# The last copy and the output's DMA move to ScalarE

## The chip, the core and the metric

The kernel runs on one core of one Trainium2 chip. The core has five engines with programs of their own: TensorE (PE in the profile), VectorE (DVE), ScalarE (ACT), GpSimd (POOL) and SyncE (SP). SP computes nothing; here it issues DMAs. Engines wait for each other through semaphores. The metric is the device time of one execution in microseconds (us); lower is better.

## What is computed

Two inputs of 640 values each pass one step of attention with a cached history (32 heads, 4096 positions, 128 values per head) and one feed-forward block, and a gate mixes the two:

```python
g = _sigmoid((x * gate_w).sum(-1, keepdims=True))
q = (x @ wq)                                   # 2 x 32 heads x 128
scores = einsum("bhqd,bhkd->bhqk", q, k_cache) * Dh ** -0.5
a = einsum("bhqk,bhkd->bhqd", softmax(scores), v_cache) @ wo
b = einsum("bsf,fd->bsd", silu(einsum("bsd,df->bsf", x, w1)), w2)
return g * a + (1 - g) * b                     # (2, 1, 640)
```

All is float32. The caches are 2 x 128 MiB; with the weights some 298 MB are read once, and 5 KB are written.

## The kernel before

The work on the caches is cut into 16 items: 8 groups of 4 heads for each of 2 inputs. An item has a K part and a V part of 8 MiB each. On-chip memory holds three such slabs, `a` and `b` for K and `v` for V, and SP issues the loads into them as they come free. For an item, POOL and DVE multiply K by the query, DVE reduces the products to scores and finds their maximum, ACT makes the exponentials, PE multiplies them with V, and DVE and PE bring the sums into the layout that the output projection needs (tile `oP`). After the last V part SP has also issued the loads of `wo` in six pieces (`load_wo`).

The end of the program is short. `in_halves` multiplies the first three quarters of `wo` into one PSUM bank; `merge` copies that bank to on-chip memory on ACT (L568) and adds it into a second bank, `acc`; `in_quarters` (L586) multiplies the last quarter of `wo`, whose pieces land last, into `acc`. Then DVE copies `acc` (160 values on each of 128 partitions) to the tile `ot` (L891), SP issues the DMA of `ot` to the output, and SP waits for its landing (L897). POOL waits until SP says that the DMA is sent and clears the kernel's semaphores (L904, L905).

Every instruction is recorded with what it reads and writes in a small class, `Flow`. `plan` finds for every operation which others it must wait for, and leaves out what its engine knows already through earlier waits. `run` then emits each engine's program in order, so all DMAs have the line of one helper, L69. `repeat` emits some PE work as a loop. `once` wraps a stretch of an engine's operations in a loop that runs one time, with a branch hint at its head; `spans` says which operations of ACT, DVE and PE are wrapped.

Near the start the program writes the output once with zeros: a DMA of 5 KB from the still zeroed tile `oP`, on SP's queue, behind the loads of `w1`, `x`, the gate, `w2` and `wq`. The tile `xz_col`, which the change uses in its place, is zeroed by POOL at L323; DVE later copies the turned input into it (L424).

The program is stored in order for each engine and loaded by DMA in pieces, here called code pages. The trace shows such loads as DMA packets of the kind "instruction".

Of the kernel before, what the change touches and what calls it, by code (L numbers as in the profile page):

```python
# [158 lines left out]
def gated_decode(nc, x, kc, vc, wq, wo, w1, w2, gate, out):  # L159
    P = 128  # L160
# [15 lines left out]
    HB = 16  # L176
    CV = 68
    G = 4
    W = D // G
    W2 = D // 2  # L180
    NP = HQ // 2
    PR = 2 * Q
# [7 lines left out]
    s_out, s_sent = nc.alloc_semaphore("output"), nc.alloc_semaphore("sent")  # L190
    f = Flow(nc)
    V, S_, T_, G_ = nc.vector, nc.scalar, nc.tensor, nc.gpsimd

    def sb(name, shape, align=32):
        return nc.alloc_sbuf_tensor(name, shape, F32, align_bytes=align)[tuple([slice(None)] * len(shape))]

    def bank(name):
        return nc.alloc_psum_tensor(name, [P, 512], F32)[:, :]
# [6 lines left out]
    def part(n, *ks):  # L205
        return [f"{n}.{k}" for k in (ks or range(8))]
# [10 lines left out]
    xz_col = sb("xz_col", [P, J * 32 + 48])  # L217
    xz, col = xz_col[:, : J * 32].rearrange("p (j z) -> p j z", z=32), xz_col[:, J * 32 :]
# [21 lines left out]
    oP, xs = oP_xs[:, : -D // Q], oP_xs[:, -D // Q :]  # L240
# [4 lines left out]
    ps_q, ps_o, ps_v, ps_acc, ps_t, ps_m, ps_0, ps_1 = (bank(f"ps{i}") for i in range(8))  # L245
    oT = ps_m[:64, 256:512].rearrange("p (n r) -> p n r", r=32)
    early, acc = ps_acc[:, :W2], ps_0[:, :W]
# [11 lines left out]
    ot = slab["v"][:, (NP - 1) * PD + W2 :][:, :W]  # L259
# [24 lines left out]
    def load_wo(g):  # L284
# [12 lines left out]
        for k, (c0, c1) in enumerate(zip(cuts, cuts[1:])):  # L297
# [12 lines left out]
        writes=part("v", 0),  # L310
# [7 lines left out]
            out=ident, in_=ident, compare_op=ALU.not_equal, fill=1.0, base=0, pattern=[[-1, P]], channel_multiplier=1  # L318
        ),
        reads=["ident"],  # L320
        writes=["ident"],
# [3 lines left out]
    f.op("POOL", lambda: G_.memset(seq, 0.0), writes=["seq"])  # L325

    out_rows = out.rearrange("b s (n d) -> (s n) b d", n=G)
    f.dma("SP", out_rows, oP[0:P:HB, :W], reads=["oP"], writes=["out"])

    f.op("DVE", lambda: V.memset(ones, 1.0), writes=["ones"])  # L330
    f.op(
# [2 lines left out]
        reads=["ident"],  # L334
        writes=["block"],
# [6 lines left out]
        reads=["block"],  # L342
        writes=["fold"],
# [4 lines left out]
        reads=["ident"],  # L348
        writes=["sel"],
# [4 lines left out]
        reads=["ident"],  # L354
        writes=["half"],
# [9 lines left out]
        reads=["sel"],  # L365
        writes=["pick"],
# [4 lines left out]
        reads=["sel"],  # L371
        writes=["own"],
# [4 lines left out]
        reads=["ident"],  # L377
        writes=["side"],
# [6 lines left out]
        reads=["block"],  # L385
        writes=["spread"],
# [4 lines left out]
        reads=["ident"],  # L391
        writes=["mask"],
    )
    f.op("DVE", lambda: V.memset(join, 0.0), writes=["join"])
    for e in range(2):
# [6 lines left out]
            reads=["ident", "join"],  # L402
            writes=["join"],
        )
        for t in (at, at + 32):
# [3 lines left out]
                reads=["ident", "join"],  # L409
                writes=["join"],  # L410
# [10 lines left out]
        reads=["xs0", "xs1"],  # L421
        writes=["xt"],
# [5 lines left out]
        reads=["xt"],  # L428
        writes=["gx"],
# [7 lines left out]
    for b in range(B):  # L437
        for j in range(J):
# [12 lines left out]
                reads=part("a") + ["xt"],  # L451
                writes=[f"hsum{b}"],
            )

    def mm_hr():
# [18 lines left out]
        reads=["ones", "gp"],  # L474
        writes=["ps_o"],
# [7 lines left out]
        reads=["g"],  # L483
        writes=["gc"],
# [7 lines left out]
    for e in range(2):  # L492
# [3 lines left out]
            reads=["ps_v"],  # L496
            writes=[f"spaced{e}"],
# [8 lines left out]
        reads=["he", "gc"],  # L506
        writes=["he"],
    )
    for e in range(2):
# [5 lines left out]
            reads=["he", "turned", "half", "seq"],  # L515
            writes=[f"seq{e}"],
# [63 lines left out]
    def in_quarters(g):  # L580
        for k in range(PR):
            at = LEAD + 32 * (g * PR + k)

            def fn(k=k, at=at):
                for n in range(G):
                    last = T_.matmul(  # L586
                        acc[32 * n : 32 * n + HB + 1, :],
                        oP[:, at : at + HB + 1],
                        slab["b"][:, k * D + n * W : k * D + (n + 1) * W],
                        start=False,  # L590
                        stop=(k == PR - 1),
                    )
                return last

            f.op("PE", fn, reads=part("b", (k >= FIRST) + (k == PR - 1)) + heads(g), writes=["ps_0"])
# [47 lines left out]
    for u in range(2):  # L643
        for b in range(B):
# [7 lines left out]
                reads=[f"ps_{u}", "mask"],  # L652
                writes=[f"qall{u}{b}"],
# [234 lines left out]
        in_halves(g_)  # L888
    merge()
    in_quarters(NP - 1)  # L890
    f.op("DVE", lambda: V.tensor_copy(ot, acc), reads=["ps_0"], writes=["ot"])  # L891
    f.dma("SP", out_rows, ot[0:P:HB, :], reads=["ot"], writes=["out"], signal=s_out)


    def land():
        nc.sync.sem_inc(s_sent)
        return nc.sync.wait_ge(s_out, 16).then_inc(s_out, -16)  # L897

    f.op("SP", land).signal = "sent"

    def clear():
        ids = sorted(s.num for s in f.sems)
# [8 lines left out]
    f.plan()  # L911
    for e in ("SP", "POOL"):
        f.run(e)
    spans = {"ACT": (14, 34), "DVE": (100, 220), "PE": (len(f.ops["PE"]) - NP * PR - 1, len(f.ops["PE"]))}
    for e, (a, b) in spans.items():
        ops, at = f.ops[e], 0
        while at < len(ops):
# [35 lines left out]
```

## Time and profile before

| what | time |
|---|---|
| median of 3 runs | 696.02 us (695.62 to 696.61) |
| the profiled execution | 695.71 us |
| its span, first to last instruction | 694.2 us |
| DMA over the span | 430 GB/s, 298.33 MB |
| DVE busy | 507.5 us (73%) |
| POOL, PE, ACT busy | 265.6, 211.4, 40.0 us |

The span runs from the first to the last instruction that the profile shows; 695.71 - 694.2 = 1.51 us lie around it. A row of the timeline gives the start in us, the duration in us, the engine, the line, the operation, the output and inputs by name, and how often; brackets hold the idle time of the engine just before, and what ended it. "SPq" is SP issuing a DMA. The chain of waits is followed back from the last instruction to what released each step.

### The profile page before, as it was taken

How to read it: one execution, taken by the hardware profiler on the slowest of the kernel's cores; microseconds unless marked ns; L12 is line 12 of the kernel's file. 1: busy time of each engine (PE TensorE's matmuls, PEld its weight loads, DVE VectorE, ACT ScalarE, POOL GpSimd, SP SyncE). 2: the span in 40 equal slices, each digit the busy share in tenths (PEclk: the TensorE clock that was granted, in tenths of full speed). 3: DMA queues.
4: the chain of work that ended last, by engine and by line, in shares of the span. 5: the costliest groups of instructions: out<-in, count | busy, mean ns of one | idle time of the engine just before them, and what ended most of it. 6: DMA issues, size and time to landing. Idle time of an engine off the chain costs nothing. (4 is left out here: it accounts for less than half of the span.)

```text
span 694.2 us, 3593 instructions
## 1 busy us (share of the span) xinstructions
PE 211.4 (30%) x1440; PEld 72.5 (10%) x1440; DVE 507.5 (73%) x269; ACT 40.0 (6%) x152; POOL 265.6 (38%) x26
## 2 busy tenths in 40 slices
PE   0074032151331405060412306060503315050657
PEld 0032010010110101020100101010100101010113
DVE  3810958898989596886959596986959595977811
ACT  0001010101010101010010101010000101010000
POOL 1000808191726090815335180906244270907100
PEclk9998556565565757575665757575655757575689
DMA  9999999999999999999999999999999999999997
GB/s 383 430 446 450 430 427 424 423 457 438 427 430 423 430 461 427 434 423 423 438 457 427 430 423 427 464 430 430 423 423 461 434 430 427 423 438 457 427 408 326
DMA packets 6209, 298.33 MB, mean 430 GB/s; under 512 B 672, under 2 KB 700, under 8 KB 956
## 3 DMA queue, kind: packets, MB, share of 16 engines
q1 hardware_dynamic: 6204, 298.27, 99.4%
q8 instruction: 2, 0.03, 0.0%
q14 instruction: 3, 0.02, 0.0%
HBM read 298.26 MB, written 0.01 MB: 430 GB/s over the span
## 5 line engine op out<-in xcount | busy, mean ns | idle before, releaser
L670 POOL TENSOR_TENSOR slabs<-slabs,qsb 128x7680 f32<-128x7680 f32 x16 | 262.3, 16396 | 378.7 <-DMA slabs<-in_A_k_cache_dram 347.8
L686 DVE TENSOR_REDUCE s<-slabs 128x68 f32<-128x8704 f32 (+1 forms) x32 | 276.3, 8676 | 0.0
L766 PE MATMUL ps<-slabs,pz 128*32 128x512 f32 x1024 | 146.2, 735 | 345.2 <-PEq L145 338.2
L676 DVE TENSOR_TENSOR slabs<-slabs,ps 128x8704 f32<-128x8704 f32 x16 | 147.5, 9218 | 108.5 <-DMA slabs<-in_A_k_cache_dram 108.4
L766 PEld LDWEIGHTS ps<-slabs,pz 128*32 128x32 f32 x1024 | 39.5, 132 | 438.6 <-issue 431.6
L715 ACT ACTIVATE pz<-s,nb 32x128 f32<-32x128 f32 x64 | 25.4, 398 | 556.5 <-PE ps L766 363.2
L804 PE MATMUL ps<-osb,pick 128*128 128x512 f32 x32 | 20.4, 724 | 58.9 <-PEq L145 58.0
L818 DVE TENSOR_REDUCE row<-ps 64x128 f32<-64x512 f32 x16 | 10.9, 682 | 23.3 <-PE ps L804 23.3
L788 DVE SCALAR_TENSOR_TENSOR osb<-ps,rg,own 128x512 f32<-128x512 f32 x16 | 12.0, 748 | 21.4 <-PE ps L766 21.2
L618 PE MATMUL ps<-qall,spread 128*128 (+1 forms) x32 | 7.4, 319 | 35.3 <-PEq L145 34.5
L446 DVE SCALAR_TENSOR_TENSOR slabs<-slabs 128x1728 f32<-128x1728 f32 x8 | 16.1, 2019 | 0.3
L458 PE MATMUL ps<-slabs,xz_col 128*32 128x432 f32 x16 | 3.1, 928 | 33.2 <-DVE slabs L446 33.2
L804 PEld LDWEIGHTS ps<-osb,pick 128*128 128x128 f32 x32 | 5.4, 211 | 73.0 <-issue 71.2
L715 ACT ACTIVATION_READ_ACCUMULATOR pz<-s,nb 32x1 f32 x64 | 11.8, 184 | 0.0
L618 PEld LDWEIGHTS ps<-qall,spread 128*128 128x128 f32 x32 | 6.9, 224 | 44.9 <-issue 43.2
L533 PE MATMUL ps<-slabs,seq 128*32 128x320 f32 x54 | 10.3, 545 | 3.7 <-DVE seq L512 3.7
L825 DVE STREAM_TRANSPOSE ps<-row 64x256 f32<-64x256 f32 x16 | 10.3, 642 | 0.6
L608 PE MATMUL ps<-slabs,xz_col 128*32 128x512 f32 x80 | 9.8, 593 | 0.0
L891 DVE COPY slabs<-ps 128x160 f32<-128x160 f32 x1 | 0.3, 325 | 12.2 <-PE ps L586 12.2
L556 PE MATMUL ps<-slabs,oP_xs 128*32 128x320 f32 x96 | 8.8, 433 | 1.4 <-DMA slabs<-in_A_wo_dram 1.4
L740 PE MATMUL ps<-rs,fold 128*128 128x1 f32 x32 | 6.1, 260 | 2.3 <-PEq L145 2.1
L740 PEld LDWEIGHTS ps<-rs,fold 128*128 128x128 f32 x32 | 5.7, 222 | 5.0 <-issue 3.5
(63 smaller groups left out, 71.9 us busy)
## 6 DMA issues: line engine op xcount, KB each, us to landing
slabs<-in_A_wq_dram SPq DMA_DIRECT2D x1, 10240.0 KB, 44.5
slabs<-in_B_w_dram SPq DMA_DIRECT2D x2, 4320.0 KB, 17.0
slabs<-in_A_wo_dram SPq DMA_DIRECT2D x1, 5120.0 KB, 21.5
slabs<-in_A_wo_dram SPq DMA_DIRECT2D x2, 1280.0 KB, 25.4
slabs<-in_A_wo_dram SPq DMA_DIRECT2D x1, 1600.0 KB, 30.1
slabs<-in_A_wo_dram SPq DMA_DIRECT2D x1, 640.0 KB, 31.1
slabs<-in_A_wo_dram SPq DMA_DIRECT2D x1, 320.0 KB, 31.4
slabs<-in_A_k_cache_dram SPq DMA_DIRECT2D x16, 47.8
```

What stands on the lines that cost most here:

```text
L446: lambda b=b, j=j, at=at: V.scalar_tensor_tensor(hsum[:, b, :], w1t[:, j, :], at, hsum[:, b, :], op0=ALU.mult, op1=ALU.add)
L533: last = T_.matmul(early[to : to + 32, :], seq[:, k : k + 2, :].rearrange("p k z -> p (k z)"), slab[n][:, k * HD : (k + 1) * HD], start=(k ...
L618: return T_.matmul(ps_q[:, :DH], spread, qall.rearrange("p h b d -> p (h b) d")[:, i, :], start=True, stop=True,)
L670: lambda: G_.tensor_mul(k[:, CV:, :], k[:, CV:, :], qsb[:, None, :].to_broadcast([P, C - CV, DH])),
L676: lambda: V.tensor_mul(k[:, :CV, :], k[:, :CV, :], ps_q[:, None, :DH].to_broadcast([P, CV, DH])),
L686: lambda c0=c0, c1=c1: V.reduce_sum(Ss[i % 2][:, c0:c1], k[:, c0:c1, :], axis=AX.X),
L715: last = S_.activation(pz[lo:hi, :, 4 * q : 4 * q + 4], s[lo:hi].rearrange("p (g c) -> p g c", c=4), AF.Exp, bias=nb[lo:hi], scale=SCALE, ...
L740: lambda *_: T_.matmul(ps_t[:, :1], fold.rearrange("p a q c -> p (a q c)"), rs, start=True, stop=True),
L766: last = T_.matmul(ps_v[32 * q : 32 * q + 32, :], pz[:, gr, :], v[:, gr, :], start=(gr < 4), stop=(gr >= NG - 4),)
L788: lambda: V.scalar_tensor_tensor(osb, ps_v.rearrange("p (c d) -> p c d", d=DH), rg, own[:, :, None].to_broadcast([P, 4, DH]), op0=ALU.mult ...
L804: lambda *_: T_.matmul(ps_o, pick, osb.rearrange("p c d -> p (c d)"), start=True, stop=True),
L818: lambda: V.reduce_sum(row, ps_o[:64].rearrange("p (c d) -> p d c", d=DH), axis=AX.X),
```

## The change

The copy of `acc` to `ot` is made by ACT in place of DVE, and ACT issues the output's DMA on its own queue. ACT also gives the signal that the DMA is sent; SP only waits for the landing. The early write of zeros moves to ACT's queue too, and reads `xz_col` in place of `oP`. As that adds one operation at the head of ACT's list, the wrapped stretch of ACT is moved by one, so that it holds the same operations. With these edits the last copy is the first slot behind a code page boundary of ACT's program.

```diff
     out_rows = out.rearrange("b s (n d) -> (s n) b d", n=G)
-    f.dma("SP", out_rows, oP[0:P:HB, :W], reads=["oP"], writes=["out"])
+    f.dma("ACT", out_rows, xz_col[0:P:HB, :W], reads=["xz"], writes=["out"])
...
     in_quarters(NP - 1)
-    f.op("DVE", lambda: V.tensor_copy(ot, acc), reads=["ps_0"], writes=["ot"])
-    f.dma("SP", out_rows, ot[0:P:HB, :], reads=["ot"], writes=["out"], signal=s_out)
-
-
-    def land():
-        nc.sync.sem_inc(s_sent)
-        return nc.sync.wait_ge(s_out, 16).then_inc(s_out, -16)
-
-    f.op("SP", land).signal = "sent"
+    f.op("ACT", lambda: S_.copy(ot, acc), reads=["ps_0"], writes=["ot"])
+    f.dma("ACT", out_rows, ot[0:P:HB, :], reads=["ot"], writes=["out"], signal=s_out)
+
+
+    f.op("ACT", lambda: S_.sem_inc(s_sent)).signal = "sent"
+    f.op("SP", lambda: nc.sync.wait_ge(s_out, 16).then_inc(s_out, -16)).signal = "sent"
...
-    spans = {"ACT": (14, 34), "DVE": (100, 220), "PE": (len(f.ops["PE"]) - NP * PR - 1, len(f.ops["PE"]))}
+    spans = {"ACT": (15, 35), "DVE": (100, 220), "PE": (len(f.ops["PE"]) - NP * PR - 1, len(f.ops["PE"]))}
```

## The prediction, made blind

> **What bounds the kernel now.** I read the share of the DMA engines first, then the chain of waits, then the timeline of the last microseconds. The stretches below give the busy time of each engine, the granted clock, the DMA share and GB/s for the start, the middle, the tail behind the last V item, and the end.
>
> ```profile
> DMA packets 6209, 298.33 MB, mean 430 GB/s; under 512 B 672, under 2 KB 700, under 8 KB 956
> 0.00:48.20 48.20, 11.28 (x56) 3.96 (x58) 25.33 (x44) 1.70 (x3) 3.24 (x10) 1.00 1.00 423
> 48.20:660.00 611.80, 178.08 (x1151) 60.20 (x1147) 477.40 (x214) 37.91 (x148) 262.33 (x16) 0.63 1.00 434
> 660.00:691.60 31.60, 21.53 (x228) 8.20 (x228) 4.42 (x11) 0.43 (x1) 0.00 (x0) 0.89 0.93 398
> 691.60:694.20 2.60, 0.48 (x10) 0.13 (x8) 0.33 (x1) 0.00 (x0) 0.00 (x0) 1.00 0.02 5
> ```
>
> The DMA engines are full from the start to 691.6 us. An edit that neither moves nor delays a load can change only the last 2.6 us, where DMA falls to 5 GB/s and each engine does one thing after another. The chain of waits shows those steps:
>
> ```profile
> 659.21 30.07 DMA slabs<-in_A_wo_dram
> ...
> 691.61 0.51 PE ps L586 x8
> 692.12 0.02 issue
> 692.15 0.33 DVE slabs L891
> ```
>
> The last piece of `wo` lands, PE multiplies it until 692.12, DVE copies from 692.15 to 692.48. Two more steps follow; the first is a row of SP's timeline, the second a row of SP's waits:
>
> ```profile
> 692.50 0.58 SPq L69 DMA_DIRECT2D out_dram<-slabs  x1
> SPq L897 <- SPq L897: 1.1, 1, 1.1
> ```
>
> So the tail is 0.33 copy, 0.02 hand-over, 0.58 issue, 1.1 landing, and the span ends at 694.2. The profiled execution took 695.71 us, so 1.51 us lie around the span. It is 0.31 below the median of the runs, 696.02; I work out a difference on the profiled execution and set it on the median.
>
> **The change part by part.**
>
> *The copy.* DVE's 0.33 goes from the path and an ACT copy of 128x160 comes in. ACT has two copies out of PSUM with other widths, and only one table load in the whole run, so the copy brings no table switch:
>
> ```profile
> L640 ACT COPY qsb<-ps 128x128 f32<-128x128 f32 x16 | 4.3, 267 | 5.9 <-PE ps L618 5.8
> L568 ACT COPY slabs<-ps 128x320 f32<-128x320 f32 x1 | 0.4, 426 | 28.4 <-PE ps L556 28.4
> L477 ACT ACT_TABLE_LOAD x1 | 1.3, 1283 | 0.7 <-PEq L943 0.7
> ```
>
> Between 128 and 320 columns lie 426 - 267 = 159 ns, 0.83 ns a column. 32 columns more than the narrow one make 267 + 27 = 294 ns against 330: -0.03 us or a little more, with ends at 267 (-0.06) and 426 (+0.10). The Trainium skill, "ScalarE: Activation LUTs", section "What ACT_TABLE_LOAD costs", gives an ACTIVATE with immediate operands 186 ns and 0.833 ns a column; an estimate by it is 319 ns, which would make the term -0.01, and the two rows, being of the copy itself, are what I use.
>
> *Wake-up.* DVE starts 0.03 behind PE's end (692.12 to 692.15). ACT's L568 was released by PE in the same way; its row and PE's end before it:
>
> ```profile
> 679.39 8.81 PE L556 MATMUL ps<-slabs,oP_xs 128*32 128x320 f32 x96 [1.40 <-DMA slabs<-in_A_wo_dram]
> 688.25 0.43 ACT L568 COPY slabs<-ps 128x320 f32<-128x320 f32 x1 [28.38 <-PE ps L556]
> ```
>
> 679.39 + 8.81 = 688.20, so ACT starts 0.05 behind; 0.02 more at most. I take 0.
>
> *Hand-over from the copy to the DMA.* Before it was 0.02 between two engines. Now ACT waits for its own copy, since the DMA reads what the copy writes. No row shows that; between two engines it is 0.02, and I take 0 difference, with 0 to +0.1 as the range, the upper end from a second wait ahead of the DMA of about the wake-up times above.
>
> *The issue.* It leaves SP and comes to ACT's queue. ACT issues no DMA before. SP's rows for this shape are 0.58 and, at the start, 0.59; its cheapest and dearest issues are in the second and third rows:
>
> ```profile
> 4.18 0.59 SPq L69 DMA_DIRECT2D out_dram<-oP_xs  x1
> L69 SPq DMA_DIRECT2D slabs<-in_A_k_cache_dram x16: 327/432/442, 33.2 to 580.3; - x16
> L69 SPq DMA_DIRECT2D oP_xs<-in_A_x_dram x1: 730/730/730, 1.9 to 1.9; - x1
> ```
>
> The ends are 0.33 and 0.73, so -0.25 to +0.15; same shape, same data, so I take 0. The landing, 1.1, is a write of the same 5 KB when the DMA engines have nothing else (5 GB/s above): 0. Nothing on ACT stands behind this wait but the signal to POOL, which follows the issue as before. SP has nothing left but the wait for landing.
>
> *The early write of zeros.* It leaves SP's queue, where it stood behind all weights, for ACT's. SP saves 0.59 at 4.18, which is nothing: its next issue waits for DVE until 33.22. On ACT it waits for POOL's memset of `xz_col` and finds ACT idle until 36.91:
>
> ```profile
> 2.44 0.27 POOL L323 MEMSET xz_col<- 128x208 f32 x1
> 36.91 0.17 ACT L477 ACTIVATE ge<-ps 128x2 f32<-128x2 f32 x1 [34.90 <-PE ps L473]
> ```
>
> So it is issued from about 2.75 to 3.4. It adds a wait: DVE's copy into `xz_col` (L424) must not overwrite what the DMA still reads. Behind that copy stands all of DVE's work on `w1`, whose end releases the first K load:
>
> ```profile
> 13.75 0.46 DVE L420 STREAM_TRANSPOSE slabs<-oP_xs 128x160 f32<-128x160 f32 x1 [7.72 <-DMA oP_xs<-in_gate_w_dram]
> 14.25 0.18 DVE L424 COPY xz_col<-slabs 128x10 f32<-128x10 f32 x1
> 3.71 0.43 SPq L69 DMA_DIRECT2D slabs<-in_A_wq_dram  x1
> 33.22 0.34 SPq L69 DMA_DIRECT2D slabs<-in_A_k_cache_dram  x1
> slabs<-in_A_wq_dram SPq DMA_DIRECT2D x1, 10240.0 KB, 44.5
> ```
>
> The load of `wq` is issued at 3.71 and lands 44.5 later, at 48.2. The K load queues behind it, so DVE may slip by about 48.2 - 33.2 = 15 us before the DMA engines run empty. With its own queue the zeros can land as early as 3.4 + 1.1 = 4.5; the nearest row on the late side is the input, which sits behind `w1` and lets DVE start at 13.75, before L424. Cost 0; cover gone, each us past 15 costs one.
>
> *Code pages.* This is the step with an open price. The kinds of DMA packets in two stretches show two loads of code in the last 5 us; the first row belongs to 690.2 to 690.6, the second to 692.6 to 693.0, and the third is DVE's last instruction before its copy:
>
> ```profile
> q14 instruction: 1, 0.01, 4.8%
> ...
> q14 instruction: 1, 0.01, 4.8%
> ...
> 679.68 0.23 DVE L837 SCALAR_TENSOR_TENSOR oP_xs<-ps,side,oE 64x8 f32<-64x8 f32 x1
> ```
>
> Between 660 and 690 only PE, DVE until 679.9 and ACT moved; ACT's L568 at 688.25 is its last instruction, and behind it its program runs on into the closing code. I read the load at 690.2 as ACT crossing its code page boundary right behind L568, which is where the change puts the copy. Then the copy's slot is reached at 688.25 as before, its page is read by 690.6, and the copy is not wanted until 692.15: 1.55 us to spare. The cover is PE's wait for the last pieces of `wo`. The load at 692.6 fits DVE running past its own last copy at 692.15; in the changed program DVE is past its last instruction at 679.9, and that load is hidden. Moving the start of ACT's wrapped stretch by one keeps the same operations in it: 0.
>
> Sum: -0.03 copy, 0 for all else: 695.71 - 0.03 = 695.68 in the profiled execution, and 696.02 - 0.03 = 695.99, say 696.0, for the median. Bounds without rivals: -0.06 - 0.25 = -0.31, and 0.10 + 0.02 + 0.1 + 0.15 = +0.37: 695.7 to 696.4.
>
> **The rivals.**
>
> *ACT waits for its code page (slower).* Place: ahead of the copy. From 688.25 to 690.6 the load took up to 2.35 us; no view shows how long after its packet the first instruction of the page can start. It decides from the point where that takes over 1.55 us. If ACT asks for the page only when PE has released it, the whole comes on the path: 0.45 to 0.85 us with the DMA engines empty, as the load at 692.6 to 693.0 came behind 692.15, up to 2.35 as at 688.25. So +0.5 to +2.35, 696.5 to 698.4. For it: the load came behind ACT's last instruction, so the page was not there ahead of time. Against it: ACT has nothing else to wait on there, and the load did start without PE. The Trainium skill, "Runtime: NRT & Kernel Launch", section "Instruction fetch mechanics", says that the next page is fetched while the current one runs, so that a crossing is mostly hidden; by that rule the copy would cost nothing extra, and the packet at 690.2, so late, does not show a page fetched well ahead. Chance 0.17, of it 0.12 above 0.2%.
>
> *DVE's late code load was on the path (faster).* If the closing 1.51 us wait for the load at 692.6, hiding it gains from 0.85 (692.15 to 693.0) to all 1.51: 694.5 to 695.1. Against: SP waits for the landing until 694.2, later than the load. Chance 0.07, of it 0.04 above 0.2%.
>
> *The zeros land late.* If they landed as late as behind `wq`, 48.2, DVE would begin L424 at 48.2 and the K load go out 19 us later, at 67: 19 us of empty DMA, 715. It decides from a landing at about 29 us. Chance 0.02.
>
> *ACT's queue is dearer.* The queue has then stood idle since 3.4 us. If issue and landing took twice their 1.7 us, 697.7. The first issue of SP, also on a queue not used before, is among its cheaper ones at 0.38 (row below), which speaks against. Chance 0.04, of it 0.03 above 0.2%.
>
> ```profile
> 0.74 0.38 SPq L69 DMA_DIRECT2D slabs<-in_B_w_dram  x1
> ```
>
> **How the numbers follow.** 0.2% is 1.39 us, about what a measurement of this kernel can tell from no change. The hidden case has 0.70, all within it. Slower: 0.12 + 0.02 + 0.03, and 0.02 for what I have not thought of: 0.19. Faster: 0.04 and 0.01 likewise: 0.05. The rest, 0.76, is within. The predicted time is 696.0. The range goes down to 695.2, which holds the issue's lower bound, the spread of the runs (695.62 at the lowest) and the near end of the faster rival, and up to 697.9, which holds most of the code page rival; the hidden case alone is 695.7 to 696.4.
>
> **What would show each step right or wrong.** In the trace after: an ACT copy of about 0.29 at 692.15, an ACT issue of about 0.58 at 692.5, and the span's end near 694.2. If the copy starts over 0.1 behind PE's last matmul, the code page rival holds, and its size is that gap. A code load near 680 and none at 692.6 would show that the late one was DVE's. DVE's L424 should still start at 14.25 and the K load go out at 33.22; an L424 that waits for a DMA to the output would be the third rival. An issue or a landing that differs from 0.58 and 1.1 is the fourth.

## The result, and where the time went

The changed kernel takes 698.38 us (median of 6 runs, 698.18 to 699.3) against 696.04 for the kernel before (6 runs): a ratio of 1.0034, 95% interval 1.0021 to 1.0047, or 2.34 us more. That is above the predicted range and on the slower side.

The page of the changed kernel has nearly the same busy times and a longer span. The two rows are its span and the busy time of each engine:

```profile
span 696.3 us, 3592 instructions
...
PE 211.4 (30%) x1440; PEld 72.5 (10%) x1440; DVE 507.2 (73%) x268; ACT 40.3 (6%) x153; POOL 265.6 (38%) x26
```

The chain of waits of the changed kernel, its last rows, has the same steps as before, with ACT in DVE's place:

```profile
658.89 30.55 DMA slabs<-in_A_wo_dram
...
691.76 0.51 PE ps L586 x8
692.28 0.02 issue
692.30 0.29 ACT slabs L891
```

The timeline then gives the issue, and the rows by line give what stands behind it: SP's wait for the landing (L896), ACT's signal that the DMA is sent (L895), and POOL's clear (L902). These last three take 17 to 243 ns; the figures behind the comma ("694.3 to 694.3") are when they started.

```profile
692.62 0.57 ACTq L69 DMA_DIRECT2D out_dram<-slabs  x1
L896 SPq EVENT_SEMAPHORE  x1: 17/17/17, 694.3 to 694.3; - x1
L895 ACTq EVENT_SEMAPHORE  x1: 17/17/17, 696.0 to 696.0; - x1
L902 POOLq EVENT_SEMAPHORE_RANGE_CLEAR  x1: 243/243/243, 696.1 to 696.1; - x1
```

In the kernel before, the same signal came from SP, and the clear followed it at once:

```profile
L896 SPq EVENT_SEMAPHORE  x1: 17/17/17, 693.1 to 693.1; - x1
L905 POOLq EVENT_SEMAPHORE_RANGE_CLEAR  x1: 243/243/243, 693.2 to 693.2; - x1
```

So the output is not late at all: PE's end moved by 0.16 us (692.12 to 692.28), the copy is 0.04 us shorter, the issue takes 0.57 in place of 0.58, and the landing is there at 694.3, where the span of the kernel before ended at 694.2. What is late is a signal that carries no data. ACT finishes the issue at 692.62 + 0.57 = 693.19 and gives the next, trivial signal at 696.0, 2.8 us later. POOL waits for it, and POOL's clear is now the end of the span: 696.3 in place of 694.2. Of the 2.47 us between the two profiled executions (698.18 and 695.71) the other 0.4 lie around the span; what they are spent on no row shows.

The chain of waits does not name that step, because it ends at the last copy; only the rows of the two signal lines show it. ACT's standing still is not an idle time in any group either: the signal is no busy work, and no group follows it.

### The profile page after: what moved, and what is told of

Same layout as the page of the kernel before. It is cut to its first block, busy times and chain, and to the rows that moved or that the text cites. A ratio compares the mean times of both kernels' runs of the same rounds, so it can differ in the third digit from the quotient of the medians.

```text
span 696.3 us, 3592 instructions
## 1 busy us (share of the span) xinstructions
PE 211.4 (30%) x1440; PEld 72.5 (10%) x1440; DVE 507.2 (73%) x268; ACT 40.3 (6%) x153; POOL 265.6 (38%) x26
## 5 line engine op out<-in xcount | busy, mean ns | idle before, releaser
L420 DVE STREAM_TRANSPOSE slabs<-oP_xs 128x160 f32<-128x160 f32 x1 | 0.5, 465 | 8.5 <-DMA oP_xs<-in_gate_w_dram 8.5
```

## The experiments

The part of an engine that reads its program is called its sequencer here, and a slot is the place of one instruction in that program. Theory A: ACT's sequencer stands still because the next piece of its program is not on the chip and must be loaded. Theory B: a semaphore instruction on ACT behind its own DMA waits for that DMA, wherever it stands.

### Moving the place, the signal and the hint

```diff
 pad1:      one more instruction at the head of ACT's program
+    pads = f.sem("pads")
+    f.op("ACT", lambda: S_.sem_inc(pads)).signal = "sent"
 sp_sends:  the signal from SP, behind the landing
-    f.op("ACT", lambda: S_.sem_inc(s_sent)).signal = "sent"
-    f.op("SP", lambda: nc.sync.wait_ge(s_out, 16).then_inc(s_out, -16)).signal = "sent"
+    def land():
+        nc.sync.wait_ge(s_out, 16).then_inc(s_out, -16)
+        return nc.sync.sem_inc(s_sent)
+    f.op("SP", land).signal = "sent"
 no_zeros:  one fewer instruction at the head of ACT's program
-    f.dma("ACT", out_rows, xz_col[0:P:HB, :W], reads=["xz"], writes=["out"])
 no_hint0:  no wrapped stretch, so no branch hint, on ACT
-    spans = {"ACT": (15, 35), ...
+    spans = {"ACT": (9999, 9999), ...
```

pad1 and no_zeros also shift the wrapped stretch so that it holds the same operations; no_zeros leaves out the early write of zeros, which the result does not need.

> The changed kernel with one more instruction at the head of ACT's program (a semaphore increment that nobody waits for), so that L568 and not the last copy is the first slot behind the code page boundary. Theory A: the crossing comes at L568, near 688.4, and the load is done before PE releases the last copy: the signal goes out right behind the DMA near 693.2, 696.0. Theory B: the place in the program plays no part, 698.4.

> The changed kernel, but SP gives POOL the signal, behind the landing, and ACT gives none. Theory A (a load of ACT's code holds ACT behind its output DMA, wherever the next slot is): POOL's clear no longer waits for ACT and starts at about 694.3, but ACT still stands for 2.8 us ahead of its closing code, so only part comes back: 697.5 to 698.0. Theory B (a semaphore instruction on ACT behind its own DMA waits until that DMA's write has come back, code plays no part): without that instruction nothing holds ACT, 696.0 to 696.5.

> The changed kernel without the early write of zeros: one ACT instruction less, so the output's DMA is the first slot behind the boundary, and ACT's queue is used for the first time at the end. Theory A: the crossing comes one slot later, the hold stays on the path, 698.2 to 699.0, with the stop ahead of the DMA or of the signal. Theory B: 698.4. If an unused queue costs, the issue or the landing is longer than 0.57 and 1.1.

> The changed kernel without the wrapped stretch on ACT: four to six slots fewer, no branch hint. Copy, DMA and signal lie ahead of the boundary. Theory A: the signal goes out at 693.2 and POOL is in time; the crossing lies in ACT's closing code, where it is either done ahead (696.0) or holds ACT until about 696 (697.5 to 698.0). Theory B: 698.4.

| run | median us | ratio to before | interval | span | around the span |
|---|---|---|---|---|---|
| before | 696.04 | | | 694.2 | 1.5 |
| the change | 698.38 | 1.0034 | 1.0021 to 1.0047 | 696.3 | 1.9 |
| pad1 | 695.83 | 0.9998 | 0.9989 to 1.0008 | 694.3 | 1.6 |
| sp_sends | 697.76 | 1.0023 | 1.0013 to 1.0032 | 694.8 | 2.9 |
| no_zeros | 697.90 | 1.0023 | 1.0013 to 1.0032 | 694.6 | 3.5 |
| no_hint0 | 695.74 | 0.9995 | 0.9985 to 1.0004 | 694.3 | 1.3 |

"Around the span" is the profiled execution's time less its span. The ratios of the experiments are against runs of the kernel before made beside them, with a median of 695.93 us in place of 696.04. One more instruction at the head of a program, doing nothing, takes the whole loss away: theory B falls, and the place in the program is shown to matter. The first load of code in pad1 comes earlier than I expected, at 663.2 and not near 688.4. Here is the signal in pad1, and, for the stretch from 660 to 694, the row of its code loads:

```profile
L898 ACTq EVENT_SEMAPHORE  x1: 17/17/17, 693.2 to 693.2; - x1
...
q14 instruction: 2, 0.02, 0.1%
```

In the changed kernel there is no load of code at all between 120 and 693.2; for 693.2 to 696.6 its rows are these, and the load on q14 falls at 694.3, while ACT stands still (693.19 to 696.0):

```profile
q8 instruction: 1, 0.02, 2.5%
q14 instruction: 1, 0.01, 0.6%
```

The loads on q14 move with ACT's program from run to run, and I take those as ACT's; the profile does not say whose they are. The other, on q8, appears also in a run that lost nothing (pad2, below) and is absent from three that lost time (sp_sends, and dve_copy and sp_dma below), so it is not what costs.

sp_sends and no_zeros split the loss. In both, the signal to POOL is in time or nearly so (694.4 and 693.9), the span is almost that of before, and yet the execution is 1.8 to 2.0 us longer, with more of it around the span (2.9 and 3.5 against 1.5). The load of ACT's code comes at 694.6 and 694.8, 1.3 and 0.9 us behind ACT's last instruction of the kernel, much as in the change (693.19 and 694.3). I read this as the same hold, now ahead of ACT's closing code and outside the span, where no row shows the hold itself. On that reading a held ACT costs about 2 us even when nothing of the kernel waits for it, because the execution waits for ACT to close.

no_zeros missed my expectation in two ways. It did not become slower than the change, and the hold was neither ahead of the DMA nor of the signal but behind both. That says that the missing slot is not the one that the words of the change name, the last copy's.

### Which slot is held

```diff
 sent_first: the two instructions behind the copy change places
+    f.op("ACT", lambda: S_.sem_inc(s_sent), reads=["ot"]).signal = "sent"
     f.dma("ACT", out_rows, ot[0:P:HB, :], reads=["ot"], writes=["out"], signal=s_out)
-    f.op("ACT", lambda: S_.sem_inc(s_sent)).signal = "sent"
 dve_copy:   the last copy goes back to DVE
-    f.op("ACT", lambda: S_.copy(ot, acc), reads=["ps_0"], writes=["ot"])
+    f.op("DVE", lambda: V.tensor_copy(ot, acc), reads=["ps_0"], writes=["ot"])
 no_hint4:   no_hint0, and at the head of ACT's program
+    pads = f.sem("pads")
+    for _ in range(4):
+        f.op("ACT", lambda: S_.sem_inc(pads)).signal = "sent"
 pad2:       pad1 with two increments
+    for _ in range(2):
+        f.op("ACT", lambda: S_.sem_inc(pads)).signal = "sent"
```

> The changed kernel with the two ACT instructions behind the last copy in the other order: the signal to POOL first, then the output's DMA. Theory A, place in the program: the hold sits ahead of the second slot behind the copy, whatever stands there. The signal goes out near 692.65 and the DMA is held for 2.8 us, to about 695.4; the landing moves with it, 698.5 to 699.0. Rival C, behind a DMA: ACT is held by something that follows each of its DMAs. The DMA goes out at 692.7, and only ACT's closing code is held: 697.5 to 698.0.

> The changed kernel with the last copy back on DVE; ACT only issues the DMA and signals, one slot earlier than in the change. Theory A: the signal is now ahead of the slot that is held and goes out at 693.2; ACT's closing code is held instead, about 2.5 us: 697.4 to 698.0. Rival C: the signal is still held behind the DMA, 698.4.

> The changed kernel without the wrapped stretch on ACT, and with four increments that nobody waits for at the head in its place, so that as many recorded ACT instructions stand ahead of the last copy as in the changed kernel. Theory A with the hint as cause of the late load: the code page is loaded near 235 us, as in the run without the stretch, and nothing is held: 695.7 to 696.0. Theory A with the place alone as cause: the hold is back, 698.4.

> The changed kernel with two more instructions at the head of ACT's program. Theory A: as with one more, the load of code is asked for while L568 waits, near 660 us, and nothing is held behind it: 695.7 to 696.1, span 694.2 to 694.4. Rival C: 698.4.

sent_first took 699.01 us (1.0045, 1.0031 to 1.0059), dve_copy 698.11 (1.0031, 1.0021 to 1.0041) and no_hint4 695.88 (1.0003, 0.9993 to 1.0012); sent_first and dve_copy are just above what theory A gave them (699.0 and 698.0 at most). The single run of pad2 took 695.76 against 695.81, too few for an interval. The timeline of sent_first, its copy and its DMA, its row for the signal, and dve_copy's row for the signal:

```profile
692.29 0.29 ACT L891 COPY slabs<-ps 128x160 f32<-128x160 f32 x1 [3.45 <-PE ps L586]
695.22 0.57 ACTq L69 DMA_DIRECT2D out_dram<-slabs  x1
...
L892 ACTq EVENT_SEMAPHORE  x1: 17/17/17, 692.6 to 692.6; - x1
...
L895 ACTq EVENT_SEMAPHORE  x1: 17/17/17, 693.3 to 693.3; - x1
```

In sent_first the signal, now one slot behind the copy, goes out at once, and the DMA, now two slots behind, is held by 2.6 us. In dve_copy the DMA and the signal both stand one slot earlier, and neither is held (692.70 and 693.3); the loss is then around the span, so by the same reading as above it is the closing code that is held. In no_zeros, likewise one slot earlier, the same. These three and the change agree on one place: the first slot that is not there is the second behind the last copy of the change. By these runs the code page ends two slots later than the change's description has it. Rival C falls: by it the signal would have been held in dve_copy, and the DMA would not have been in sent_first.

no_hint4 has as many recorded ACT instructions ahead of the copy as the change, and is not slow. The wrapped stretch is therefore what makes the load late. no_hint4's row of code loads from 120 to 688 shows it; no_hint0 has the same one, and the changed kernel has none there:

```profile
q14 instruction: 1, 0.01, 0.0%
```

In no_hint0 that load lies in the window from 234 to 240, inside the time that the wrapped stretch spans in the changed kernel (167.6 to 390.0). Without the stretch the next code page is fetched then, over 450 us ahead of its use; with it that load does not come, and the fetch is left until the sequencer gets to the missing slot. That the stretch keeps the fetch from coming is shown by the load being there or not. Whether that is due to the branch hint or to the loop that the hint stands in is not shown: no run has one without the other. How the sequencer decides is not shown either.

### When the load is asked for, and the copy alone

Why did pad1 load its page while L568 waited, near 660 us, and the change not while the last copy waited? I supposed that ACT's sequencer reads on past copies that wait for PE, but stops at an instruction whose wait it must carry out itself.

```diff
 late_pad: the added increment stands between L568 and the last copy, and waits for L568
+    f.op("ACT", lambda: S_.sem_inc(pads), reads=["partial"]).signal = "sent"
     f.op("ACT", lambda: S_.copy(ot, acc), reads=["ps_0"], writes=["ot"])
 sp_dma:   ACT keeps the copy, SP issues the output's DMA and signals
-    f.dma("ACT", out_rows, ot[0:P:HB, :], reads=["ot"], writes=["out"], signal=s_out)
+    f.dma("SP", out_rows, ot[0:P:HB, :], reads=["ot"], writes=["out"], signal=s_out)
... (the signal from SP, as in the kernel before)
```

> The changed kernel with one more instruction, not at the head but between L568 and the last copy: an increment that nobody waits for and that waits until L568 has written. The DMA thereby comes to the recorded place at which all held runs were held, as in the run with one more at the head. Theory A with decoding ahead (ACT's sequencer reads on past copies that wait for PE, but stops at a wait that the sequencer itself carries out, as a signal or a DMA issue is): it stops at the added increment until 688.9, then asks for the page; the load of code is at 690 to 691 in place of 663, and is done just about when the copy ends, so 695.7 to 696.5. Rival D (the load is asked for at a fixed slot, whatever waits): the load is near 663 as in the run with one more at the head.

> The changed kernel with the output's DMA and the signal back on SP; ACT keeps the copy as its last instruction. Theory A: output, landing and signal are on time (landing 694.2 to 694.4), but ACT's closing code reaches the missing page only behind the copy, near 692.6, and is held for 2.5 to 2.8 us, to about 695.3; the closing then ends 0.9 to 1.1 us later than in the kernel before: 696.8 to 697.1. Rival (only work that stands behind the DMA on ACT matters): 695.9.

late_pad took 695.82 us (0.9997, 0.9987 to 1.0006). It has as many slots ahead of the DMA as pad1, and the added instruction runs at 688.9, when L568 is done. Its code load, for the window 688 to 691, and pad1's, for the window 660 to 666:

```profile
q14 instruction: 1, 0.01, 0.6%
```

```profile
q14 instruction: 1, 0.01, 0.3%
```

The packets lie at 690.0 and 663.2. So with the same place in the program the load comes 27 us later when the sequencer has something to stop at, and rival D, a fixed slot, falls. No row shows where the sequencer stands; what follows is the reading that fits the packets. In pad1 it reads past L568 and the last copy, which both wait for PE, up to the DMA, and asks for the DMA's page near 660. In the change the DMA is the last slot of the page: the sequencer gets to it early, stops there because the DMA waits for the copy, and touches the missing slot only at 693.19. It had 33 us to spare and could not use them. A fixed number of slots read ahead would not give this: in pad1 the DMA stands two slots behind L568, the one that waits, and in the change the missing slot stands two behind the last copy, which waited from 688.8 to 692.30, yet the load came only at 694.3.

sp_dma took 696.76 us (1.0010, 1.0000 to 1.0019), just below the 696.8 to 697.1 expected, and its interval begins at 1, so the loss is barely clear of the noise. With DMA and signal on SP a good third of the loss stays, as it should if the copy on ACT alone leaves ACT's closing code to be held. The load on q14 comes at 693.5, 0.6 us behind the copy. The copy and the issue are not held:

```profile
692.64 0.29 ACT L891 COPY slabs<-ps 128x160 f32<-128x160 f32 x1 [3.46 <-PE ps L586]
692.95 0.60 SPq L69 DMA_DIRECT2D out_dram<-slabs  x1
```

None of the mended versions beats the kernel before: pad1, late_pad, no_hint0 and no_hint4 all have intervals that take in 1. Copy and issue on ACT, with the code in place, are worth nothing that these runs can tell from zero.

## Why the prediction was wrong

- *The copy, wake-up, hand-over, issue and landing* were right. The copy is 0.29 (forecast 0.294), starts 0.02 behind PE's end, the issue on ACT is 0.57 (forecast 0.58), and the landing is at 694.3, near the forecast 694.2. For the issue that was partly luck: it was set at SP's 0.58 for the same shape, but no_zeros, where it is the first on ACT's queue, has 1.15, and only the early zeros make it the second. Had the code been in place, the forecast of 696.0 would have held: pad1 measured 695.83, no_hint4 695.88.
- *The early write of zeros* cost nothing, as forecast, though its issue took 1.22 (forecast 0.59) and L424 started later than forecast: it ran at 15.06 and the first K load went out at 34.03, 0.81 later, well within the 15 us of cover. The input had landed later (L420 at 14.56), and L424 follows L420 by 0.50 in both kernels, so it did not wait for the zeros. Nor did the zeros delay the input: L420 starts at 13.90 in pad1, which has them on ACT, and at 13.94 in no_zeros.

```profile
14.56 0.47 DVE L420 STREAM_TRANSPOSE slabs<-oP_xs 128x160 f32<-128x160 f32 x1 [8.53 <-DMA oP_xs<-in_gate_w_dram]
15.06 0.18 DVE L424 COPY xz_col<-slabs 128x10 f32<-128x10 f32 x1
34.03 0.34 SPq L69 DMA_DIRECT2D slabs<-in_A_k_cache_dram  x1
```

- *Code pages* is the step that failed: "Then the copy's slot is reached at 688.25 as before, its page is read by 690.6, and the copy is not wanted until 692.15: 1.55 us to spare." I took the load at 690.2 in the kernel before as coming at the copy's slot. The runs put it two slots later. (Right behind L568 is not the copy's place in any case, since with the early zeros at its head L568 itself stands one slot further on.) In the kernel before, ACT ran on into its closing code behind L568, which ended at 688.68, so it reached the missing slot by itself, at about 689 if the packet at 690.2 came some 1.1 us behind, as in the change. In the change two instructions that depend on PE's end stand in between, and the DMA's own wait keeps the sequencer from it: its page is not read by 690.6 but from 694.3, and ACT is held from 693.19 to 696.0.
- In the same step I gave the load at 692.6 to DVE. The changed kernel has no load near 681, where DVE is then done; dve_copy, with the last copy on DVE from 692.35 to 692.68, has none between 691 and 693.3; and late_pad, with the last copy on ACT, has both. Its row for the window 691 to 693:

```profile
q14 instruction: 1, 0.01, 1.0%
```

  So the load at 692.6 too is most likely ACT's, the page after the next.
- *The issue* step ended with "Nothing on ACT stands behind this wait but the signal to POOL, which follows the issue as before." The signal was named and priced at nothing without its cover: what hides it is that its instruction is on the chip. That cover was gone, and POOL's clear and the closing stand behind it.
- The rival "ACT waits for its code page" had the right mechanism and chance 0.17, and the wrong place: "ahead of the copy". So its check, a gap between PE's end and the copy, would have told against it; the copy started on time. Its price, 0.5 to 2.35 us, came from the time between request and packet; measured, ACT was held 2.6 to 2.8 us, as the time from the packet to the first instruction, which I noted as not shown by any view, adds to it. The measured 2.34 us lie at its upper end, and the range was cut below that; the agreement is chance, as the 2.35 was the time from L568 to a packet, and the loss is what a hold of 2.8 us behind the issue leaves.
- The rule that I set beside it, from the Trainium skill, "Runtime: NRT & Kernel Launch", section "Instruction fetch mechanics", that the next page is fetched while the current one runs and a crossing is mostly hidden, describes no_hint0, with its load over 450 us ahead. It does not describe the changed kernel, where the wrapped stretch stands in that place and no load comes until 694.3.

## What to carry to other kernels

When an edit makes an engine's program longer or moves its last operations, find where that engine's code loads fall (the DMA packets of kind "instruction") and what stands between the last wait and the missing slot: a signal or the closing code can be held for some 2.7 us where no chain of waits shows it. By the reading that fits these runs, ACT reads on past copies that wait for PE, but not past a signal or a DMA issue that waits, so a load is hidden only if no such wait stands ahead of the crossing (663.2 in pad1, 690.0 in late_pad, 694.3 in the change). A loop with a branch hint can put off the fetch of the next page. Moving the program by one do-nothing instruction is a cheap test of whether a loss comes from there.

## What the runs showed that I had not expected

The first DMA issue on an engine's own queue was dear on ACT and not on SP. On ACT the first took 1.22 at 2.73 us and the later one 0.57; without the early zeros the only one, at the end, took 1.15, where SP's first issue of all took 0.38.

```profile
2.73 1.22 ACTq L69 DMA_DIRECT2D out_dram<-xz_col  x1
...
692.76 1.15 ACTq L69 DMA_DIRECT2D out_dram<-slabs  x1
```

The first row is of the changed kernel, the second of no_zeros. The landing moved much less than the issue: in no_zeros the span ends 694.6 - 692.44 = 2.2 us behind the copy's start, in the change the landing comes 694.3 - 692.30 = 2.0 behind it.

And a crossing that finds its page in place may not be quite free: in no_hint4 the signal comes at 693.7, where the issue ends at 692.85 + 0.56 = 693.41, some 0.3 us, against nearly none in pad1 (693.16 and 693.2). That the crossing lies just there in no_hint4 is not shown.

What stays open: why the count of slots in the change's words and in the runs differs by two, whose the load on q8 in the last microseconds is, and whether the hint or its loop puts the fetch off, and by what rule.
